# One attention unit programmed ahead, a third load slot, row sums from a column of ones, more small buffers

## The chip, the cores and the metric

One core of a Trainium2 chip runs the kernel as one program. The metric is device time in microseconds from the runs of the kernel; lower is better. The profile is of one execution. TensorE is PE in its rows (PEld its weight loads), VectorE DVE, ScalarE ACT, GpSimd POOL, SyncE SP; SP issues all the kernel's DMAs.

## The reference

Causal attention and a linear memory are mixed by a gate and fed to a two-layer network (called MoE in the code, with one expert). Shapes: B, H, S, D = 4, 8, 576, 64; 2304 tokens of 512 features; the hidden layer is 2048 wide.

```python
def _attn_ref(q, k, v, M_prev, z_prev, beta):
    scores = scale * np.matmul(q, k.transpose(0, 1, 3, 2))
    scores = np.where(causal, -1000000000.0, scores)
    scores = scores - scores.max(-1, keepdims=True)
    a = np.exp(scores)
    a /= a.sum(-1, keepdims=True) + 1e-09
    local = np.matmul(a, v)
    q_p = phi(q)                       # elu + 1
    mem_ret = np.einsum('bhsd,bhde->bhse', q_p, M_prev)
    mem_norm = np.einsum('bhsd,bhd->bhs', q_p, z_prev)[..., None] + 1e-06
    g = 1.0 / (1.0 + np.exp(-beta))[None, :, None, None]
    return g * (mem_ret / mem_norm) + (1 - g) * local

def reference(**kwargs):
    x = attn_out.transpose(0, 2, 1, 3).reshape(B * S, H * D)
    r = np.maximum(x @ w_in, 0.0)
    return (r * r) @ w_out
```

## The kernel before

All is float32 in and out; most matmuls run on float16 halves: a value is split into a high half and the rest, and a product takes three matmuls (high x high, high x low, low x high).

**Attention** runs in 24 units, in the order of the list `order`. A unit is one batch b, one pair of heads p and some query tiles. A tile is 128 queries (numbers 1 to 4); the first 64 tokens of each batch are handled apart at the start. Batches 0 and 1 have units of tiles 1 and 2 (four pairs), then of tiles 3 and 4 (four pairs); batches 2 and 3 have units of all four tiles. So units 0 to 7 are batch 0, 8 to 15 batch 1, 16 to 19 and 20 to 23 batches 2 and 3. A unit consists of a start and of rows.

The start: `loads` (L417, L421, L424) brings k, then q with the memory matrix (qm), then v (vv) into slots of which there are two each. q and k are split (qh, ql, kh, kl: L444 to L451), except in units 0 to 5, which use float32 scores; phi of q is made in place (L461 to L467). From unit 3 on v is scaled by a power of two that its largest absolute value gives: a maximum per partition (vx, L483), one small matmul that spreads it (vt, L487), a maximum and a reciprocal (vy, L488 to L492), vz (L493), and the split into vh and vl in the tile vs (L498, L500). Units 0 to 2 use v as it is. Then the memory product pm (L520), its norm (nm) and the first write of feat, the unit's 128 features of the tokens (L531). Then `after()` issues the loads of the next unit.

The rows, in the tile order 2, 1, 3, 4: scores (sp, L554, with a raised priority), a masked copy with the row minimum of the negated scores (e and mx, L575), the exponential (L595), which also sums its row into sm by the accumulator output, the split of the weights into float16 halves (a: L633 on ScalarE, L635 on VectorE), a transposing DMA (aT, L639), the factor of the row (sm times vz, reciprocal: L640, L644), the products with v (acc, L659), and the update of feat (L662). sm and mx have four buffers, vx, vy, vz and nm two.

PSUM is shared by names: up (2 buffers), acc (2), av (2) and s. vt, pm and the acc of attention all use the two av buffers.

Units above the fourth take their big tiles by turns from two pools, at for even units and the late pool (`more[-1]`) for odd ones, one buffer each of qh, ql, kh, kl, vs.

**MoE** runs in blocks of 256 tokens, `moe(n)`: up matmuls (L936 to L938), relu and square (L942, L943), the halves gh and gl (L945, L948), down matmuls (L908 to L910), output. Block 0 are the first tokens; blocks 1 to 6 follow; the tokens of the last two are done together in `moe_last` by a scheme of seven products (L782 to L784, L811). A block starts from `token_halves`: squares, scale and halves of feat (hl, two buffers) and a transposing DMA.

**What sets the order.** Each engine's queue is a fixed list. The program's order gives the priority, and a scheduler at build time lays the instructions out from it with modelled durations: an instruction later in the program can move forward when its inputs and its buffer are there. `ORD` writes attention units 0 to 3 merged with the weights' loading and conversion and with block 0, then units 4 to 23 one after the other, and behind these the MoE blocks; so MoE matmuls of a batch that is done fill TensorE beside later units. Within the attention part the program has a unit's start, its rows, the next unit's start, its rows.

## Time and profile before

| | us |
|---|---|
| runs of the kernel | 583.03, 586.88, 589.49 (median 586.88) |
| the profiled execution | 584.98 |
| its span, first to last instruction | 583.2 |
| TensorE busy | 535.7 (92%) |
| VectorE busy | 455.7 (78%) |
| ScalarE busy | 397.2 (68%) |
| GpSimd busy | 59.7 (10%) |
| mean granted TensorE clock, share of full | 0.97 |

A row of the waits gives the engine and line, what released it, the total, the number of waits and the longest. A busy TensorE is not one at its peak: its matmuls overlap, and their ends are modelled.

### The profile page before, as it was taken

How to read it: one execution, taken by the hardware profiler on the slowest of the kernel's cores; microseconds unless marked ns; L12 is line 12 of the kernel's file. 1: busy time of each engine (PE TensorE's matmuls, PEld its weight loads, DVE VectorE, ACT ScalarE, POOL GpSimd, SP SyncE). 2: the span in 40 equal slices, each digit the busy share in tenths (PEclk: the TensorE clock that was granted, in tenths of full speed). 3: DMA queues.
4: the chain of work that ended last, by engine and by line, in shares of the span. 5: the costliest groups of instructions: out<-in, count | busy, mean ns of one | idle time of the engine just before them, and what ended most of it. 6: DMA issues, size and time to landing. Idle time of an engine off the chain costs nothing.

```text
span 583.2 us, 12895 instructions
## 1 busy us (share of the span) xinstructions
PE 535.7 (92%) x4903; PEld 380.4 (65%) x4903; DVE 455.7 (78%) x1413; ACT 397.2 (68%) x853; POOL 59.7 (10%) x41
## 2 busy tenths in 40 slices
PE   6578997799799899999998999988999999999997
PEld 6466774576577576657765766656676776446766
DVE  6988779998687686889895775989767769795735
ACT  2566886777688677869787866889566664556452
POOL 2760674010010000000000000000000000000000
PEclk9968998699999999999998999999999999999999
DMA  8921886345865643767546846569454335100002
GB/s 308 404 89 38 281 320 164 90 100 121 157 128 117 143 118 91 158 136 174 123 108 104 196 74 118 117 122 178 64 114 86 79 57 71 38 0 1 2 1 72
DMA packets 131022, 70.87 MB, mean 122 GB/s; under 512 B 113296, under 2 KB 119440, under 8 KB 130960
## 3 DMA queue, kind: packets, MB, share of 16 engines
q1 hardware_dynamic: 130960, 70.05, 50.6%
q8 instruction: 38, 0.62, 0.5%
q14 instruction: 24, 0.20, 0.1%
HBM read 37.53 MB, written 4.72 MB: 72 GB/s over the span
## 4 chain that ended last, share of the span: by engine, by line
PE 35%; DVE 21%; ACT 12%; DMA 10%; issue 4%; SPq 1%; POOLq 0%; DVEq 0%; ACTq 0%
DVE a L635 4%; PE oacc L909 4%; PE oacc L908 4%; PE oacc L910 4%; PE up L938 4%; PE up L936 4%; PE up L937 4%; DMA qm<-in_qv_dram 3%; DVE e L575 3%; ACT e L595 3%; DMA vv<-in_qv_dram 3%; PE seven L811 3%; DMA aT<-a 3%; PE acc L659 3%; PE sp L554 2%
## 5 line engine op out<-in xcount | busy, mean ns | idle before, releaser
L936 PE MATMUL up<-xT,w 128*128 128x256 f16 x448 | 123.1, 275 | 1.2 <-ACT r L942 1.2
L937 PE MATMUL up<-xT,w 128*128 128x256 f16 x448 | 123.1, 275 | 0.3 <-DVE xT L397 0.3
L938 PE MATMUL up<-xT,w 128*128 128x256 f16 x448 | 123.2, 275 | 0.0
L595 ACT ACTIVATE e<-e,mx 128x320 f32<-128x320 f32 (+3 forms) x128 | 77.4, 606 | 46.3 <-DVE feat L662 27.4
L908 PE MATMUL oacc<-w,gh 128*128 128x512 f16 x224 | 85.5, 382 | 2.2 <-ACT gh L945 2.1
L635 DVE SCALAR_TENSOR_TENSOR a<-e,a 128x128 f16<-128x128 f32 x116 | 64.8, 569 | 27.3 <-ACT a L633 26.4
L909 PE MATMUL oacc<-w,gh 128*128 128x512 f16 x224 | 85.4, 381 | 0.0
L910 PE MATMUL oacc<-w,gl 128*128 128x512 f16 x224 | 81.0, 380 | 1.3 <-DVE gl L948 1.2
L633 ACT ACTIVATE a<-e 128x128 f16<-128x128 f32 x116 | 54.9, 523 | 3.9 <-DMA aT<-a 2.4
L659 PE MATMUL acc<-vs,aT 128*128 128x64 f16 x1138 | 46.3, 195 | 11.7 <-DMA aT<-a 7.2
L659 PEld LDWEIGHTS <-aT 128*128 128x128 f16 x1138 | 41.5, 99 | 20.8 <-DMA aT<-a 10.2
L937 PEld LDWEIGHTS <-w 128*128 128x128 f16 x448 | 44.3, 99 | 11.5 <-issue 1.5
L938 PEld LDWEIGHTS <-w 128*128 128x128 f16 x448 | 44.2, 99 | 9.2 <-issue 1.2
L936 PEld LDWEIGHTS <-w 128*128 128x128 f16 x448 | 44.2, 99 | 9.2
L575 DVE CUSTOM_DVE_ANT_0 e<-sp,mask 128x320 f32<-128x320 f32 (+3 forms) x128 | 47.0, 417 | 1.5 <-PE sp L554 1.0
L193 POOL TENSOR_SCALAR raw<-raw 128x512 uint32<-128x512 uint16 x21 | 44.8, 2134 | 21.4 <-DMA raw<-in_w_in_dram 12.8
L948 DVE TENSOR_TENSOR gl<-r,gh 128x512 f16<-128x512 f32 x56 | 39.4, 704 | 7.3 <-ACT gh L945 6.9
L942 ACT ACTIVATE r<-up,gam 128x512 f32<-128x512 f32 x48 | 32.3, 674 | 18.2 <-PE up L938 18.2
L910 PEld LDWEIGHTS <-gl 128*128 128x128 f16 x224 | 21.4, 98 | 23.5 <-DVE gl L948 3.4
L811 PEld LDWEIGHTS <-g 128*128 128x128 f16 x336 | 32.6, 98 | 6.0 <-DVE g L737 1.8
L908 PEld LDWEIGHTS <-gh 128*128 128x128 f16 x224 | 22.0, 98 | 22.1 <-ACT gh L945 2.7
L943 ACT ACTIVATE r<-r 128x512 f32<-128x512 f32 x56 | 34.9, 624 | 0.8
(196 smaller groups left out, 1076.1 us busy)
## 6 DMA issues: line engine op xcount, KB each, us to landing
raw<-in_w_in_dram SPq DMA_DIRECT2D x16, 512.0 KB, 7.1
raw<-in_w_out_dram SPq DMA_DIRECT2D x16, 512.0 KB, 7.9
vv<-in_qv_dram SPq DMA_DIRECT2D x16, 320.0 KB, 3.2
kd<-in_kk_dram SPq DMA_DIRECT2D x16, 288.0 KB, 3.2
out_dram<-o SPq DMA_DIRECT2D x12, 256.0 KB, 2.4
qm<-in_qv_dram SPq DMA_DIRECT2D x8, 321.0 KB, 3.4
qm<-in_qv_dram SPq DMA_DIRECT2D x8, 193.0 KB, 2.9
vv<-in_qv_dram SPq DMA_DIRECT2D x8, 192.0 KB, 4.7
```

What stands on the lines that cost most here:

```text
L575: nc.vector.tensor_tensor_reduce(out=e[:, h, ka:kb], in0=sps[:, h, cs], in1=mask[:, 448 - q0 + ka : 448 - q0 + kb], scale=-0.125, scalar=3 ...
L595: ex = nc.scalar.activation(e[:n, h, :ke], e[:n, h, :ke], AF.Exp, bias=bs, scale=-1.0, accum_out=sm[:n, h : h + 1])
L633: nc.scalar.mul(av[:, :, o0 : o0 + w], x, SC)
L635: nc.vector.scalar_tensor_tensor(out=av[:, :, o0 + w : o0 + 2 * w], in0=x, scalar=SC, in1=av[:, :, o0 : o0 + w], op0=ALU.mult, op1=ALU.sub ...
L659: nc.tensor.matmul(acc[:n, h], lhs[:, :n], rhs, start=x == 0, stop=x == len(mms) - 1)
L811: mms.append(nc.tensor.matmul(x[:, blk], g[j][:, i0, a, blk, p], t_side(j, p, m, i1), start=j == js[0] and p == n == 0, stop=j == js[-1] a ...
L908: nc.tensor.matmul(acc[t], gh[:, u, ts], w_out_op(f, 0), start=f == f0, stop=False)
L909: nc.tensor.matmul(acc[t], gh[:, u, ts], w_out_op(f, 1), start=False, stop=False)
L910: nc.tensor.matmul(acc[t], gl[:, u, ts], w_out_op(f, 0), start=False, stop=f == f1)
L936: nc.tensor.matmul(up[:, u, :], w_in_op(f, k, 0), xT[:, :, k], start=k == 0, stop=False)
L937: nc.tensor.matmul(up[:, u, :], w_in_op(f, k, 0), xT[:, :, NK + k], start=False, stop=False)
L938: nc.tensor.matmul(up[:, u, :], w_in_op(f, k, 1), xT[:, :, k], start=False, stop=k == NK - 1)
```

## The change

A unit's start of the program stands before the rows of the unit ahead of it: from unit 4 on (`FIRST`), `attn` runs the start of unit i + 1 up to a mark ("whole"), and then the rows of unit i. From unit 8 on (`AHEAD`) the loads go round three slots, the third one in the late pool, and from the start of unit 6 on loads are issued up to two units ahead instead of one. The tile of v (vs) has a column of ones behind vh, made once per pool; the products with vh are 65 columns wide and give the row sums, so that the exponential has no accumulator output except in units 0 to 2, and the factor sm is made after acc. The order of the three products changes. vx, vy, vz and nm get four buffers, mx and sm eight, hl four in the late pool; the last block's halves get tiles of their own.

```diff
-QB = 2
-VVB = 2
+LO = D + 2
-KB = 2
+AHEAD = 8
@@ before loads
+    def with_ones(ap):
+        if ap not in ones:
+            ones[ap] = ap.tile([P, 2, 5, LO + D], F16, tag="vs", name="vs", bufs=1)
+            nc.vector.memset(ones[ap][:, :, :, D : D + 1], 1.0)
+        return ones[ap]
-    def loads(b, p, tiles):
+    def loads(i):
+        b, p, tiles = order[i]
+        n = i % 2 if i < AHEAD else i % 3
+        lp = at if n < 2 else more[-1]
...
-        kd = at.tile([P, S], F32, tag="kd", name="kd", bufs=KB)
+        kd = lp.tile([P, S], F32, tag=f"kd{n}", name="kd")
...
-        qm = at.tile([P, 2 * ZW + SQ], F32, tag="qm", name="qm", bufs=QB)
+        qm = lp.tile([P, 2 * ZW + SQ], F32, tag=f"qm{n}", name="qm")
...
-        vv = at.tile([P, 5 * P], F32, tag="vv", name="vv", bufs=VVB)
+        vv = lp.tile([P, 5 * P], F32, tag=f"vv{n}", name="vv")
@@ attention (vx, vy, vz, nm: bufs=2 to bufs=4; mx, sm: bufs=4 to bufs=8)
-            nc.vector.tensor_scalar(out=vz, in0=gs[:, h0 : h0 + 2], scalar1=vy, scalar2=None, op0=ALU.mult)
-            vs = ap.tile([P, 2, 5, 2 * D], F16, tag="vs", name="vs", bufs=1)
+            nc.vector.tensor_scalar(out=vz, in0=gm[:, h0 : h0 + 2], scalar1=vy, scalar2=None, op0=ALU.mult)
+            vs = with_ones(ap)
...
-            vh, vl = (vs[:, :, :ncn, i * D : (i + 1) * D] for i in range(2))
+            vh, vl = (vs[:, :, :ncn, o : o + D] for o in (0, LO))
...
         after()
+        if ap_early:
+            yield "whole"
...
-                    e[:n, h, :ke], e[:n, h, :ke], AF.Exp, bias=bs, scale=-1.0, accum_out=sm[:n, h : h + 1]
+                    e[:n, h, :ke], e[:n, h, :ke], AF.Exp, bias=bs, scale=-1.0,
+                    **({"accum_out": sm[:n, h : h + 1]} if full else {}),
...
-            nc.vector.scalar_tensor_tensor(
-                out=sm[:n], in0=sm[:n], scalar=1e-9, in1=gm[:n, h0 : h0 + 2] if full else vz[:n],
-                op0=ALU.add, op1=ALU.mult,
-            )
-            nc.vector.reciprocal(sm[:n], sm[:n])
+            if full:
...
-            acc = ps.tile([P, 2, D], F32, tag="av", name="acc", bufs=2)
+            acc = ps.tile([P, 2, LO], F32, tag="av", name="acc", bufs=2)
...
-                    vh, vl = (vs[:, h, :, x * D : (x + 1) * D] for x in range(2))
+                    vh, vl = vs[:, h, :, : D + 1], vs[:, h, :, LO:]
...
-                        mms += [(low, vh[:, c]), (hi, vh[:, c]), (hi, vl[:, c])]
+                        mms += [(low, vh[:, c]), (hi, vl[:, c]), (hi, vh[:, c])]
...
+            if not full:
+                nc.vector.scalar_tensor_tensor(
+                    out=sm[:n], in0=acc[:n, :, D], scalar=SC * 1e-9, in1=vz[:n], op0=ALU.add, op1=ALU.mult
+                )
+                nc.vector.reciprocal(sm[:n], sm[:n])
@@ token_halves
-            hl = mo.tile([P, 2 * DM], F16, tag="hl", name="hl", bufs=2)
+            hl = more[-1].tile([P, 2 * DM], F16, tag="hl", name="hl", bufs=4)
@@ the units
+    def unit(i):
+        ld = nxt.pop(0)
+        def after():
+            while i + len(nxt) + 1 < min(len(order), i + (3 if i + 2 >= AHEAD else 2)):
+                nxt.append(loads(i + len(nxt) + 1))
+        ap = more[-1] if i > FIRST and i % 2 else at
+        early = i < NEF and max(order[i][2]) < 4
+        return attention(*order[i], ld, after, i < NEARLY, i < NES, early, ap, i >= FIRST)
     def attn(i0, i1):
+        ahead = []
         for i in range(i0, i1):
-            ld = nxt.pop()
-            def after():
-                if i + 1 < len(order):
-                    nxt.append(loads(*order[i + 1]))
-            yield from attention(*order[i], ld, after, ...)
+            rows = ahead.pop() if ahead else unit(i)
+            if i >= FIRST:
+                for x in (rows,) if i == FIRST else ():
+                    for _ in iter(lambda: next(x), "whole"):
+                        yield
+                if i + 1 < i1:
+                    ahead.append(unit(i + 1))
+                    for _ in iter(lambda: next(ahead[0]), "whole"):
+                        yield
+            yield from rows
```

## Rows read from the trace of the kernel before

**Rows 1.** Busy time by stage: length, PE, PEld, DVE, ACT, POOL, clock, DMA share, GB/s.

```profile
100.00:120.00 20.00, 14.91 (x111) 10.79 (x111) 19.76 (x63) 14.25 (x29) 1.41 (x1) 0.74 0.45 103
...
115.00:300.00 185.00, 176.14 (x1678) 124.92 (x1674) 151.37 (x538) 141.08 (x321) 6.85 (x6) 1.00 0.60 128
300.00:480.00 180.00, 169.72 (x1700) 121.31 (x1699) 135.46 (x492) 129.53 (x294) 0.00 (x0) 0.99 0.57 109
480.00:583.20 103.20, 98.46 (x654) 63.41 (x652) 71.33 (x103) 51.04 (x68) 0.00 (x0) 0.99 0.12 26
```

**Rows 2.** Waits of TensorE's matmuls, 115 to 500 us: total, times, longest.

```profile
PE acc L659 <- DMA aT<-a: 7.2, 5, 2.8
PE sp L554 <- DVE ql L445: 3.0, 3, 2.3
PE oacc L908 <- ACT gh L945: 2.1, 2, 1.6
PE acc L659 <- DVE mx L575: 1.6, 1, 1.6
PE oacc L910 <- DVE gl L948: 1.2, 2, 1.0
PE up L936 <- ACT r L942: 1.2, 2, 1.0
PE sp L554 <- DVE vx L485: 1.2, 1, 1.2
PE vt L487 <- DVE feat L662: 0.7, 1, 0.7
PE acc L659 <- DVE vs L500: 0.5, 2, 0.2
```

**Rows 3.** Chain that ended last, 198 to 204 us; VectorE's timeline at 354 us.

```profile
199.49 2.91 DMA qm<-in_qv_dram
...
202.86 0.44 DVE ql L445
...
354.73 0.82 DVE L483 TENSOR_REDUCE vx<-vv 128x1 f32<-128x640 f32 x1 [2.95 <-DMA vv<-in_qv_dram]
```

**Rows 4.** Waits of ScalarE and of SP's queue, 115 to 500 us.

```profile
ACT e L595 <- DVE feat L662: 27.4, 16, 3.2
ACT qh L444 <- DMA qm<-in_qv_dram: 20.8, 12, 2.9
...
SPq L421 <- PE pm L520: 17.1, 7, 8.2
```

**Rows 5.** Timeline, 284 to 321 us, units 16 to 18: start, duration, instruction.

```profile
284.36 0.82 DVE L483 TENSOR_REDUCE vx<-vv 128x1 f32<-128x640 f32 x1 [1.56 <-DMA vv<-in_qv_dram]
...
298.71 0.60 ACT L444 CAST qh<-qm 128x512 fp32r<-128x512 f32 x1
...
306.19 0.56 ACT L595 ACTIVATE e<-e,mx 128x320 f32<-128x320 f32 x1 [2.18 <-DVE feat L662]
...
315.37 0.48 DVE L662 SCALAR_TENSOR_TENSOR feat<-acc,sm,feat 128x64 f32<-128x64 f32 x2 [1.02 <-PE acc L659]
...
317.50 0.22 PE L487 MATMUL vt<-identb,vx 128*128 128x128 bf16 x1
...
320.04 0.83 ACT L498 ACTIVATE vs<-vv,vy 128x640 f16<-128x640 f32 x1
```

**Rows 6.** Groups of instructions (count, busy us, mean ns); landing of aT.

```profile
L659 PE MATMUL acc<-vs,aT 128*128 128x64 f16 x1138 | 46.3, 195 | 11.7 <-DMA aT<-a 7.2 <-DVE vs L500 2.6 <-DVE mx L575 1.6
...
L595 ACT ACTIVATION_READ_ACCUMULATOR e<-e,mx 128x1 f32 x108 | 20.3, 188 | 0.0
...
L662 DVE SCALAR_TENSOR_TENSOR feat<-acc,sm,feat 128x64 f32<-128x64 f32 x112 | 25.6, 276 | 5.5 <-PE acc L659 5.4
L640 DVE SCALAR_TENSOR_TENSOR sm<-sm,vz 128x2 f32<-128x2 f32 x56 | 6.3, 153 | 0.4
...
DMA to landing us min/median/max: 2.8/4.1/6.7
```

More of the change, by code (lines that the diff above doesn't have):

```diff
@@ L318, in first_tokens @@
             elif step == "l":
-                nxt.append(loads(*order[0]))
+                nxt.append(loads(0))
             elif step == "g":
@@ L412, in fused_kernel @@
     feat = {}
-    def loads(b, p, tiles):
+    ones = {}
+    def with_ones(ap):
[7 more added lines that the diff above has]
+        lp = at if n < 2 else more[-1]
         qa, qb = QT[tiles[0]][0], sum(QT[tiles[-1]])
-        kd = at.tile([P, S], F32, tag="kd", name="kd", bufs=KB)
+        kd = lp.tile([P, S], F32, tag=f"kd{n}", name="kd")
         nc.sync.dma_start(kd[:, :qb], kk_d[b, p, :, :qb])
-        qm = at.tile([P, 2 * ZW + SQ], F32, tag="qm", name="qm", bufs=QB)
+        qm = lp.tile([P, 2 * ZW + SQ], F32, tag=f"qm{n}", name="qm")
         qa, qb = qa - D + 2 * ZW, qb - D + 2 * ZW
@@ L425, in loads, with attention @@
         return kd, qm, vv
-    def attention(b, p, tiles, ld, after, early, sfull, full, ap):
+    def attention(b, p, tiles, ld, after, early, sfull, full, ap, ap_early):
         q_eng, k_eng = (nc.gpsimd if c == 'p' else nc.vector for c in (EARLY if early else LATE))
@@ L478, in attention @@
         if not full:
-            vx = at.tile([P, 1], F32, tag="vx", name="vx", bufs=2)
-            vy = at.tile([P, 1], F32, tag="vy", name="vy", bufs=2)
-            vz = at.tile([P, 2], F32, tag="vz", name="vz", bufs=2)
+            vx = at.tile([P, 1], F32, tag="vx", name="vx", bufs=4)
+            vy = at.tile([P, 1], F32, tag="vy", name="vy", bufs=4)
+            vz = at.tile([P, 2], F32, tag="vz", name="vz", bufs=4)
             vc = v[:, :ncn]
@@ L522, in attention @@
                     later("t", mm)
-            nm = at.tile([P, 3, 2], F32, tag="nm", name="nm", bufs=2)
+            nm = at.tile([P, 3, 2], F32, tag="nm", name="nm", bufs=4)
             pv = pm.rearrange("p i (h z) -> p i h z", h=2)[:, :ng]
@@ L568, in scores @@
                         ap.tile([P, 2, S], F32, tag="e", name="e", bufs=EB if ap is at else EB2),
-                        at.tile([P, 2, 2], F32, tag="mx", name="mx", bufs=4),
-                        at.tile([P, 2], F32, tag="sm", name="sm", bufs=4),
+                        at.tile([P, 2, 2], F32, tag="mx", name="mx", bufs=8),
+                        at.tile([P, 2], F32, tag="sm", name="sm", bufs=8),
                     )
@@ L639, in attention @@
                 nc.sync.dma_start_transpose(out=aT[:, :, :n], in_=a[:n])
[L640 to L644 removed]
+            if full:
+                nc.vector.scalar_tensor_tensor(
+                    out=sm[:n], in0=sm[:n], scalar=1e-9, in1=gm[:n, h0 : h0 + 2], op0=ALU.add, op1=ALU.mult
+                )
+                nc.vector.reciprocal(sm[:n], sm[:n])
             yield
[L647 removed]
+            acc = ps.tile([P, 2, LO], F32, tag="av", name="acc", bufs=2)
             for h in range(2):
@@ L656, in attention @@
                         hi, low = aT[:, h * nb + c], aT[:, h * nb + i + c]
-                        mms += [(low, vh[:, c]), (hi, vh[:, c]), (hi, vl[:, c])]
+                        mms += [(low, vh[:, c]), (hi, vl[:, c]), (hi, vh[:, c])]
                 for x, (lhs, rhs) in enumerate(mms):
-                    nc.tensor.matmul(acc[:n, h], lhs[:, :n], rhs, start=x == 0, stop=x == len(mms) - 1)
+                    nc.tensor.matmul(
+                        acc[:n, h, : rhs.shape[-1]], lhs[:, :n], rhs, start=x == 0, stop=x == len(mms) - 1
+                    )
+            if not full:
+                nc.vector.scalar_tensor_tensor(
+                    out=sm[:n], in0=acc[:n, :, D], scalar=SC * 1e-9, in1=vz[:n], op0=ALU.add, op1=ALU.mult
+                )
+                nc.vector.reciprocal(sm[:n], sm[:n])
             for h in range(2):
@@ L662, in attention @@
                 nc.vector.scalar_tensor_tensor(
-                    out=xo, in0=acc[:n, h], scalar=sm[:n, h : h + 1], in1=xo, op0=ALU.mult, op1=ALU.add
+                    out=xo, in0=acc[:n, h, :D], scalar=sm[:n, h : h + 1], in1=xo, op0=ALU.mult, op1=ALU.add
                 )
@@ L717, in moe_last @@
         ss, sc, osc, gam2 = (mo.tile([P, 4], F32, name=n) for n in ("ss4", "sc4", "osc4", "gam2"))
-        hs = [tl.tile([P, 2, DM], F16, tag="g", name="xh", bufs=3) if t < 2 else mo.tile([P, 2, DM], F16, tag="hl", name="hl", bufs=2) for t in range(4)]
+        hs = [tl.tile([P, 2, DM], F16, tag="g", name="xh", bufs=3) if t < 2 else tl.tile([P, 2, DM], F16, name=f"xh{t}") for t in range(4)]
         fb = feat[B - 1]
@@ L1005, in fused_kernel @@
     if not nxt:
-        nxt.append(loads(*order[0]))
+        nxt.append(loads(0))
+    def unit(i):
[6 more added lines that the diff above has]
+        return attention(*order[i], ld, after, i < NEARLY, i < NES, early, ap, i >= FIRST)
     def attn(i0, i1):
+        ahead = []
         for i in range(i0, i1):
-            ld = nxt.pop()
-            def after():
-                if i + 1 < len(order):
-                    nxt.append(loads(*order[i + 1]))
-            yield from attention(*order[i], ld, after, i < NEARLY, i < NES, i < NEF and max(order[i][2]) < 4, more[-1] if i > FIRST and i % 2 else at)
+            rows = ahead.pop() if ahead else unit(i)
[8 more added lines that the diff above has]
+            yield from rows
             b, p, tiles = order[i]
```

## The prediction

> **What bounds the kernel now.** I read the busy time by stage first, then TensorE's own waits, then who makes the other engines late. After 115 us the matrix engine is busy 95, 94 and 95% of three long stages; the next engine, VectorE, 82, 75 and 69% [rows 1]. The attention units run down to about 480 us, and the feed-forward (MoE) matmuls fill TensorE between their pieces. The reader is to see that attention finishing sooner is by itself worth nothing: matmuls that no longer run beside it run after it. What counts after 115 us is the time in which TensorE sits in front of a matmul whose input is late. From 115 to 500 us that is nine lines, 18.7 us together: 7.2 on transposes of the softmax weights (aT), 3.0 and 1.2 in front of scores, 2.1 and 1.2 and 1.2 in front of MoE matmuls, 1.6, 0.7 and 0.5 in front of products with v [rows 2]. The stage before, VectorE full at 19.76 of 20 us while the last weights are converted and TensorE at 14.91 [rows 1], is made of weights and of early units, which the change leaves as they are.
>
> Then the causes. The longest wait in front of scores ends a chain that starts with a load: qm is issued at 199.49, takes 2.91 us, and ql follows at 202.86 [rows 3]. At 354.73 VectorE has sat 2.95 us in front of vx, whose vv was loading [rows 3]; its queue goes in order, so the gl behind it is late too. Loads are late because SP holds a qm load until the second-last unit's pm has read the slot: 17.1 us in seven waits; ScalarE in turn is idle 20.8 us in front of qh for want of qm [rows 4]. ScalarE waits 27.4 us in front of the exponentials, released by a feat update of VectorE [rows 4]. An exponential needs no feat; it writes its row sums into sm, of which there are four, and the tile four earlier is read up to its feat.
>
> Last, the order within a unit. Unit 18 casts its q at 298.71, before unit 17's first exponential at 306.19: that half of a unit's start already runs a unit ahead. The half with v does not: unit 17 has its maximum at 284.36, but vt, with one small instruction between, comes at 317.50, just behind unit 16's last feat at 315.37, and v is split from 320.04 [rows 5]. vt, pm and acc share two PSUM buffers named av, which go round in program order, and a unit's vt stands there behind the earlier unit's acc.
>
> **The change part by part.** The sum is made against the profiled execution, 584.98 us (span 583.2, 1.8 around it); it is 1.9 below the median of the runs shown, 586.88.
>
> *Third slot, loads two units ahead.* The same loads, none added; they leave SP one unit sooner, because the slot they wait for was read a unit earlier. Behind a waiting load on SP stand the transposes, and behind those acc, so SP waits less in front of both. The waits for ql (3.0) and vx (1.2) go: −4.2. Of the 1.2 in front of MoE matmuls on gl, the longest stall, 1.0, is the one at 355 us: −1.0. Bounds: 0, if the load merely waits elsewhere, and −5.4.
>
> *A unit's start before the rows of the unit ahead of it.* No instruction is added; about a dozen of VectorE and ScalarE and, on TensorE, vt and pm move in front of the earlier unit's rows. acc waiting on vs (0.5) and vt waiting on feat (0.7) go: −1.2. Bounds: 0 and −2.8, with the 1.6 on mx, which I keep, because VectorE's rows now stand behind another unit's start.
>
> *Row sums by the ones column.* The 108 reads of the accumulator in the stage go: 20.3 us of ScalarE [rows 6]. ScalarE is not the bound (76 and 72% in the attention stages [rows 1]), so this gives nothing directly. With the four sm also gone as a brake (eight now, and written only after acc), the 27.4 us of waits go. What TensorE gets is part of its 2.1 and 1.2 us on gh and r, which queue behind those exponentials: I take half, −1.6; ends 0 and −3.3. A tile of number i has 2(2 + 3i) products, 2(1 + 2i) of them with vh; 13, 13, 16 and 16 tiles of i = 1 to 4 make 720 of the 1138 [rows 6]. They get a column more: 46.3 us over 1138 x 64 columns is 0.64 ns a column, +0.5. The two instructions on sm (153 ns the first [rows 6], the second much alike) move behind acc, which holds its PSUM buffer until two feat of 276 ns are done [rows 6]: 0.55 us becomes some 0.86. TensorE's only wait on feat was 0.7, so +0.4; if every one of 58 tiles paid, +18. The wait of VectorE for acc is no new one, feat stood there before.
>
> *More small buffers, four hl in another pool, persistent v tiles, two memsets.* No instruction but the memsets is added: nothing. The MoE matmuls cover them; uncovered, two memsets of 10 columns cost less than two feat updates of 64 (276 ns [rows 6]), 0.6 us.
>
> *What gets worse.* Units no longer chained run closer. VectorE at 75% from 300 to 480 us [rows 1] lets that stage shrink by a quarter at most; I take an eighth, half of it. Transposes come 1.14 times as dense, and the 7.2 us of waits on them grow by 1.0. Their landing takes 4.1 us in the median and 6.7 at most [rows 6], so the bad end is five waits longer by 2.6 us each, +13; the good end is that all 7.2 go.
>
> The Trainium skill speaks against this part ("DMA: Bandwidth & Descriptors", section on queues, rings and completion order): descriptors from SP are consumed in ring order on each DMA engine, so a transpose stands behind loads that were sent ahead of it. By that rule the +13 would be the nearer end, 591 in all; the median of 4.1 us, with loads in the same queue already, says that most transposes don't pay it, so 579 stands.
>
> Sum: −4.2 −1.0 −1.2 −1.6 +0.5 +0.4 +1.0 = −6.1. 584.98 − 6.1 is 578.9: 579 us, 1.3% under the median shown. From the median itself the same step gives 580.8, so the forecast stands near the edge of what can be told apart: about 1% (5.9 us) is what a measurement here can tell from no change.
>
> **The rivals.** *B, nothing moves.* The score half ran ahead already [rows 5], and TensorE's stalls come where the fixed order of its queue and the real arrivals differ; the same number appears at other places. For it: two of the nine lines, on aT and mx, are of a kind that is not touched, and they are 8.8 of the 18.7 us [rows 2]. Against: loads issued just in time are named in two chains. Time: 583 to 588, middle 586.
>
> *C, VectorE becomes the bound; slower.* With the chains cut, attention, first in priority, fills VectorE; gl of the MoE blocks comes late and TensorE idles beside it; the matmuls pushed back are then paid after attention. The price by the nearest row: from 100 to 120 us VectorE was at 19.76 and TensorE lost 5.1 of 20 us [rows 1]. If half of what is left of the last attention stage (135 us of VectorE work, so 68) runs like that, it costs 17: 579 + 17 = 596. It decides where a stretch has VectorE over some 95%; at the 82% of the stage from 115 to 300 us, TensorE loses only 8.9 of 185. That is what speaks against it: the fullest long stage loses no more than the others.
>
> The Trainium skill has a rule that points the same way ("Perfetto Trace Analysis", section Optimization Strategy): where the most-contended engine changes over time, interleaving the stages helps. Running attention apart from the MoE matmuls is the contrary; by it C would be the case. The trace bears it out only in the stretch of 100 to 120 us.
>
> *D, much faster.* If all nine waits go, aT's too because their tiles are ready a unit sooner, 584.98 − 18.7 + 0.9 = 567. Against: nothing in the change shortens a transpose, and acc is still placed close behind it.
>
> **How the numbers follow.** Chances: the forecast (575 to 584) 0.50, B 0.20, C 0.18, D 0.12. The likeliest has its own range, 575 to 584: lower end with the waits on mx, gh and r gone wholly (3.3 more), upper end with the loads' 5.2 not won. The range 568 to 593 leaves out most of C (0.13) and a sliver of D (0.05). Faster by over 1% (below 581.0): D whole and two thirds of the forecast, 0.46; slower (above 592.8) nearly all of C and a little of B's spread, 0.19; the rest, 0.35, within 1%.
>
> **What would show it.** Right: SP's waits on pm before qm loads nearly gone; no ScalarE idle before qh on qm and no VectorE idle before vx on vv; no exponential waiting on feat, no accumulator reads in units after the third; vt a unit before its acc; attention done well before 480 us; TensorE's waits from 115 us on down to about 12 us, mostly aT. Wrong: the same TensorE idle total at other lines (B); VectorE above 95% with MoE matmuls waiting on gl or gh (C); aT landing at 5 us and more with acc waiting on it (the bad end of the transposes). What would break the forecast most simply is TensorE idle that grows in the attention stages while those stages get shorter.

## The result, and the profile after

The kernel after takes 590.34 us in the median of its runs (587.34 to 592.37), the kernel before 583.11 beside it (580.38 to 589.49). The ratio is 1.013, with an interval of 1.0107 to 1.0152: slower by 1.3%, where 1% faster was forecast. The profiled execution has a span of 588.5 us, 5.3 more than before; the one before, against which the forecast was made (584.98 us), lies 1.9 above its kernel's median.

The page after has TensorE busy 539.8 us (535.7 before), VectorE 459.7 (455.7), ScalarE 388.6 (397.2) and GpSimd 60.0 (59.7). Next come the stages of the kernel after, with the columns of [rows 1]; the last two rows are pieces of the stage from 115 to 300 us.

```profile
100.00:120.00 20.00, 15.24 (x102) 10.79 (x103) 16.63 (x42) 10.67 (x18) 1.41 (x1) 0.66 0.48 84
115.00:300.00 185.00, 171.42 (x1599) 120.84 (x1598) 165.03 (x587) 144.35 (x289) 5.95 (x6) 0.96 0.67 143
300.00:480.00 180.00, 174.60 (x1737) 126.28 (x1735) 130.94 (x461) 118.85 (x222) 0.00 (x0) 1.00 0.52 99
480.00:588.50 108.50, 103.97 (x690) 67.06 (x687) 66.10 (x93) 50.30 (x66) 0.00 (x0) 1.00 0.05 15
180.00:200.00 20.00, 19.88 (x196) 15.43 (x197) 19.01 (x79) 19.55 (x48) 0.00 (x0) 0.92 0.63 132
240.00:260.00 20.00, 19.35 (x176) 13.82 (x177) 19.30 (x69) 17.68 (x36) 0.00 (x0) 0.91 0.70 142
```

Against [rows 1] the reader is to see two stages that moved in opposite directions. From 300 to 480 us TensorE is idle 5.4 us, where it was 10.3: the later attention stage moved as was forecast, by 4.9 us. From 115 to 300 us it is idle 13.6, where it was 8.9, and its mean clock fell from 1.00 to 0.96. The clock stands at its lower level (1.2 GHz) in four stretches of some 3.4 us there, and in none before; at half speed they cost about half their length, an estimate of some 6.7 us. VectorE went from 151.4 to 165.0 in the same stage: more of attention runs there. In idle time the two stages about cancel, 19.0 us where it was 19.2. The 5.3 us are for the most part TensorE's own busy time, 4.1 more for the same 4903 matmuls, which is where a lower clock shows.

These are TensorE's waits from 115 to 500 us after, with the columns of [rows 2].

```profile
PE sp L567 <- DVE mx L588: 7.2, 7, 1.8
PE vt L498 <- DVE feat L683: 2.8, 3, 1.2
PE oacc L931 <- DVE gl L969: 2.7, 2, 1.9
PE sp L567 <- ACT e L608: 1.5, 2, 1.1
PE oacc L931 <- DVE vy L500: 1.3, 1, 1.3
PE acc L673 <- DVE feat L542: 1.0, 1, 1.0
PE pm L531 <- DVE feat L683: 0.9, 2, 0.7
PE acc L673 <- DMA qm<-in_qv_dram: 0.6, 1, 0.6
PE sp L567 <- DVE vy L500: 0.3, 1, 0.3
PE oacc L929 <- ACT gh L966: 0.3, 1, 0.3
```

The ten lines come to 18.6 us; before, nine lines came to 18.7 [rows 2]. The lines are mostly others. All 7.2 us on the transposes aT are gone, and so are the waits on ql, vx and vs, and those on gh and r fell from 3.3 to 0.3; in their place stand 7.2 us of scores that wait for the masked copies (mx) to empty the one PSUM buffer s, and 3.7 us of vt and pm behind a feat.

Who waits on the other engines, 115 to 500 us after, answers to [rows 4]; the last line is VectorE's wait before vx.

```profile
ACT e L608 <- DVE mx L588: 34.7, 26, 3.0
...
ACT qh L455 <- DMA qm<-in_qv_dram: 6.7, 5, 2.3
...
SPq L432 <- PE pm L531: 15.1, 5, 6.0
...
DVE vx L494 <- DMA vv<-in_qv_dram: 15.1, 13, 2.0
```

The exponentials' 27.4 us on feat are gone, and in their place they wait 34.7 us on mx (13.2 before). ScalarE's wait for q fell from 20.8 to 6.7. VectorE's wait for v hardly fell (16.8 before in the same window).

### The profile page after: what moved, and what is told of

Same layout as the page of the kernel before. It is cut to its first block, busy times and chain, and to the rows that moved or that the text cites. A ratio compares the mean times of both kernels' runs of the same rounds, so it can differ in the third digit from the quotient of the medians.

```text
span 588.5 us, 12787 instructions
## 1 busy us (share of the span) xinstructions
PE 539.8 (92%) x4903; PEld 384.0 (65%) x4903; DVE 459.7 (78%) x1415; ACT 388.6 (66%) x737; POOL 60.0 (10%) x41
## 4 chain that ended last, share of the span: by engine, by line
PE 46%; DVE 20%; DMA 18%; ACT 11%; issue 3%; SPq 1%; POOL 1%; ACTq 0%; DVEq 0%
DMA vv<-in_qv_dram 6%; PE up L957 5%; DMA aT<-a 5%; PE up L959 4%; PE up L958 4%; PE oacc L930 4%; PE oacc L931 4%; PE oacc L929 4%; PE seven L832 4%; PE acc L673 4%; DVE e L588 3%; DVE a L649 3%; PE sp L567 3%; ACT a L647 2%; PE seven L804 2%
## 5 line engine op out<-in xcount | busy, mean ns | idle before, releaser
L957 PE MATMUL up<-xT,w 128*128 128x256 f16 x448 | 125.4, 280 | 0.0
L958 PE MATMUL up<-xT,w 128*128 128x256 f16 x448 | 125.3, 280 | 0.0
L959 PE MATMUL up<-xT,w 128*128 128x256 f16 x448 | 125.3, 280 | 0.0
L608 ACT ACTIVATE e<-e,mx 128x320 f32<-128x320 f32 (+3 forms) x128 | 72.8, 607 | 41.1 <-DVE mx L588 40.8
L647 ACT ACTIVATE a<-e 128x128 f16<-128x128 f32 x116 | 54.3, 523 | 18.7 <-DMA aT<-a 18.3
L958 PEld LDWEIGHTS <-w 128*128 128x128 f16 x448 | 45.1, 101 | 11.1 <-issue 0.6
L957 PEld LDWEIGHTS <-w 128*128 128x128 f16 x448 | 45.0, 101 | 11.0
L959 PEld LDWEIGHTS <-w 128*128 128x128 f16 x448 | 45.0, 100 | 7.6 <-issue 0.4
L673 PE MATMUL acc<-vs,aT 128*128 128x65 f16 (+1 forms) x1138 | 44.7, 196 | 3.2 <-DVE feat L542 1.6
```

The lines of the kernel that those rows point to most:

```text
L608: ex = nc.scalar.activation(e[:n, h, :ke], e[:n, h, :ke], AF.Exp, bias=bs, scale=-1.0, **({"accum_out": sm[:n, h : h + 1]} if full else {}),)
L647: nc.scalar.mul(av[:, :, o0 : o0 + w], x, SC)
L673: nc.tensor.matmul(acc[:n, h, : rhs.shape[-1]], lhs[:, :n], rhs, start=x == 0, stop=x == len(mms) - 1)
L957: nc.tensor.matmul(up[:, u, :], w_in_op(f, k, 0), xT[:, :, k], start=k == 0, stop=False)
L958: nc.tensor.matmul(up[:, u, :], w_in_op(f, k, 0), xT[:, :, NK + k], start=False, stop=False)
L959: nc.tensor.matmul(up[:, u, :], w_in_op(f, k, 1), xT[:, :, k], start=False, stop=k == NK - 1)
```

## The experiments

Each ratio is to runs of the kernel before beside it, with its 95% interval. Where tiles in flight are given, they were counted in the trace: tiles whose exponential has started and whose feat has not, averaged over time.

### One part at a time

Three theories stood at first. O: starting a unit before the rows of the one ahead packs attention densely, and VectorE becomes the bound. S: sums made from acc come too late. L: the third slot crowds SP's queue.

**Rows first, start after**, everything else of the change kept:

```diff
-            if i >= FIRST:
+            if i >= LEAD:    # LEAD = 99
```

> The changed kernel with the program's order undone alone: a unit's start stands behind the rows of the unit before it again; third slot, ones column and buffers stay. Theory O (the new order packs units 4 to 15 so densely that VectorE is the bound there: in the changed kernel it is busy 165.0 of 185 us from 115 to 300 us, against 151.4 before, and TensorE loses 13.6 us in idle and about 6.7 us in half clock there against 8.9 and 0): back to 581 to 585. Theory S (row sums behind acc make VectorE wait for TensorE: 11.2 us in six waits on acc): stays at 588 to 592. Theory L (a third load slot crowds SP): stays at 588 to 592.

Measured: 596.41 us, ratio 1.0252 (1.0191 to 1.0312). Undoing the order made it 1.2% worse, so theory O does not explain the loss: within the change the build with the order is the better one. None of the three theories had 596.

**Sums by the accumulator again**, everything else kept (the eight sm too):

```diff
-                    e[:n, h, :ke], e[:n, h, :ke], AF.Exp, bias=bs, scale=-1.0,
-                    **({"accum_out": sm[:n, h : h + 1]} if full else {}),
+                    e[:n, h, :ke], e[:n, h, :ke], AF.Exp, bias=bs, scale=-1.0, accum_out=sm[:n, h : h + 1]
...
-                    vh, vl = vs[:, h, :, : D + 1], vs[:, h, :, LO:]
+                    vh, vl = vs[:, h, :, :D], vs[:, h, :, LO:]
```

> The changed kernel with the row sums undone alone: the exponential gives them by its accumulator again, and sm is made before acc. Theory S: back to 581 to 585, VectorE's 11.2 us of waits on acc go back to about 5. Theory O: 589 to 592, since 20 us more of ScalarE come back and the density stays. Theory L: 588 to 592.

Measured: 590.77 us, ratio 1.0144 (1.0099 to 1.0190). The same as the kernel after, with the waits elsewhere: 4.9 us on aT again, 1.8 on mx. Theory S is not it.

**Two slots**, everything else kept:

```diff
-AHEAD = 8
+AHEAD = 99
```

> The changed kernel with two load slots and loads one unit ahead, all else as in it. Theory L: back to 581 to 585. Theory O: 588 to 594, the order is the same, and loads come later still. Theory S: 588 to 592.

Measured: 584.83 us, ratio 1.0046 (1.0009 to 1.0082). Taking the slot out gives back some 5 us, as L wants. It also tells against VectorE as the bound: the stage from 200 to 300 us is as full of VectorE as in the kernel after (88.2 and 88.7 of 100 us), and the kernel is 5 us faster.

**The order alone**, in the code of the kernel after with its other parts undone:

```diff
+            if i >= FIRST:
+                for x in (rows,) if i == FIRST else ():
+                    for _ in iter(lambda: next(x), "whole"):
+                        yield
+                if i + 1 < i1:
+                    ahead.append(unit(i + 1))
```

> The kernel before with the program's order alone: a unit's start ahead of the earlier unit's rows; two slots, accumulator sums, small tiles, hl and v tiles as before. Theory O: 588 to 594, and from 115 to 300 us VectorE at 88% or more with TensorE losing more than before's 8.9 us. Theories S and L: 579 to 584.

Measured: 589.31 us, ratio 1.0115 (1.0071 to 1.0160). That is O's time, but not its sign: VectorE is at 83% from 115 to 300 us (154.05 of 185), where O asked for 88%. So the order costs 1.2% alone and gives about 1% inside the change. The sign depends on what else is there, and parts that change sign need another kind of theory. From here on the rivals were R (the reshuffle: each engine's queue is laid out at build time by modelled durations, any edit lays it out anew, and a new order is worth some per cent either way), P or M (the parts have prices of their own), and several narrower ones.

**Everything undone in the code of after**, sums and counts of buffers as before too:

```diff
-AHEAD = 8
+AHEAD = 99
+LEAD = 99
...
-            vs = with_ones(ap)
+            vs = ap.tile([P, 2, 5, LO + D], F16, tag="vs", name="vs", bufs=1)
```

> The code of the kernel after with every part of the change undone: rows before the next start, two slots, sums by the accumulator, the old buffer counts. What is left of the new code is the layout of the slots' names, a v tile two columns wider without ones, and the order of the last two of the three products with v; the build-time queue may come out a little different. Every theory of a part expects 583 us, within 1 of the kernel before. Theory R (reshuffle: the queues are fixed at build time by modelled durations, so any edit moves TensorE's stalls, and the time of any new order of the queues is uncertain by some 1%) allows up to 6 us either way, and the width it shows here is the width with which the other runs must be read.

Measured: 585.33 us, ratio 1.0027 (0.9997 to 1.0057). What is left of the new code costs nothing that can be told. Its stages are the base for the runs that add one part to it:

```profile
115.00:300.00 185.00, 172.32 (x1639) 122.47 (x1638) 146.94 (x523) 136.68 (x311) 6.39 (x6) 1.00 0.61 126
300.00:480.00 180.00, 173.16 (x1719) 123.37 (x1717) 139.13 (x500) 133.41 (x302) 0.00 (x0) 0.99 0.56 113
```

**The third slot alone**, against the kernel with everything undone:

```diff
-AHEAD = 99
+AHEAD = 8
```

> The kernel before with the third slot and the loads two units ahead alone. Theory P (the third slot has a price of its own, loads collide with the transposes on SP's queue): 588 to 589 us, the 5.5 us that taking it out of the kernel after gave back, with more waits of acc on aT. Theory O (it only does harm together with the order, where attention already presses on VectorE): 579 to 583, the waits on ql, vx and qm gone. Theory R: anywhere from 578 to 590, not to be worked out from the other runs.

Measured: 578.54 us, ratio 0.9931 (0.9897 to 0.9965): faster than the kernel before, and 6.8 us faster than the kernel that it differs from by the slot alone. P, which took the slot's harm for its own, is refuted. Its stages, and TensorE's waits from 115 to 500 us:

```profile
115.00:300.00 185.00, 178.07 (x1686) 126.06 (x1684) 153.75 (x552) 144.90 (x325) 6.98 (x6) 0.99 0.65 137
300.00:480.00 180.00, 173.74 (x1720) 124.42 (x1719) 133.57 (x484) 127.85 (x291) 0.00 (x0) 0.99 0.58 105
```

```profile
PE acc L673 <- DMA aT<-a: 5.7, 5, 3.5
PE acc L673 <- ACT vs L510: 2.5, 1, 2.5
PE acc L673 <- DVE feat L543: 1.2, 2, 0.6
PE sp L568 <- DVE mx L589: 1.0, 1, 1.0
PE acc L673 <- DVE vs L512: 0.8, 1, 0.8
PE acc L673 <- DVE sm L658: 0.7, 1, 0.7
PE oacc L924 <- ACT gh L961: 0.5, 1, 0.5
PE vt L499 <- DVE feat L678: 0.4, 1, 0.4
PE up L952 <- ACT r L958: 0.2, 1, 0.2
```

The waits of scores on ql are gone (3.7 us with everything undone), and the waits come to 13.0 us in all, where they are 19.2 with everything undone. VectorE does not wait before vx at all (9.2 us with everything undone). The stages idle 6.9 and 6.3 us, against 12.7 and 6.8 with everything undone and 8.9 and 10.3 in the kernel before [rows 1].

**The ones column alone**, against the kernel with everything undone:

```diff
+            vs = with_ones(ap)
...
+                    **({"accum_out": sm[:n, h : h + 1]} if full else {}),
...
+                    vh, vl = vs[:, h, :, : D + 1], vs[:, h, :, LO:]
```

> The kernel before with the row sums from the ones column alone. In the three kernels with the ones column TensorE lost 7 to 11 us in front of scores on mx and little on aT; in the three with accumulator sums it was the other way. Theory Q (the ones column is what moves the stalls from aT to mx): sp on mx at 6 us or more here, acc on aT under 4, ScalarE without waits on feat. Time by Q alone: 583 to 587, as the two waits are of like size. Theory P: no change, 583. Theory R: 578 to 590.

Measured: 593.1 us, ratio 1.0148 (1.0093 to 1.0202). Q is right on where the waits stand (scores on mx 8.9 us, acc on aT 2.0, no exponential on feat) and wrong on the time, by 6 us at least. R's range ended at 590, so it was too narrow, here and in the next three runs.

**The buffers alone**, against the same (vx, vy, vz and nm likewise from two to four):

```diff
-                        at.tile([P, 2, 2], F32, tag="mx", name="mx", bufs=4),
-                        at.tile([P, 2], F32, tag="sm", name="sm", bufs=4),
+                        at.tile([P, 2, 2], F32, tag="mx", name="mx", bufs=8),
+                        at.tile([P, 2], F32, tag="sm", name="sm", bufs=8),
...
-            hl = mo.tile([P, 2 * DM], F16, tag="hl", name="hl", bufs=2)
+            hl = more[-1].tile([P, 2 * DM], F16, tag="hl", name="hl", bufs=4)
```

> The kernel before with the larger counts of small buffers (mx, sm 8 each; vx, vy, vz, nm 4 each; four hl in the late pool) alone. Theory Q': the eight sm already free the exponentials (27.4 us of ScalarE's waits on feat gone) and scores run ahead, so sp on mx appears here without the ones column. Theory Q: it doesn't, the accumulator sums still tie exponentials to ScalarE's order; time 581 to 584. Theory R: 578 to 590, and the four single parts don't add up to the whole change's 7.2 us.

Measured: 593.74 us, ratio 1.0154 (1.0099 to 1.0208). Scores wait on mx 4.4 us, so the freed sm does some of that without the column, as Q' has it; the exponentials' waits on feat are not gone, 9.8 us are left. Order, column and buffers cost 1.2, 1.5 and 1.5% alone and the slot gives 0.7: 3.5% by sum, where the whole costs 1.3. They don't add up.

### The four sm as a brake

In every kernel with four sm and accumulator sums the tiles in flight stand at 3.6 or 3.7 in the mean after 300 us and never above 4: the four sm hold the exponentials back. In the kernel after they are 9.6 from 300 to 350 us. Theory K made this the cause.

**Eight sm alone**, against the kernel with everything undone:

```diff
-                        at.tile([P, 2], F32, tag="sm", name="sm", bufs=4),
+                        at.tile([P, 2], F32, tag="sm", name="sm", bufs=8),
```

> The kernel before with eight sm instead of four, and nothing else of the change. In the five kernels so far with four sm and accumulator sums the tiles between their exponential and their feat are 3.6 in the mean and never above 4 from 150 us on: ScalarE waits 27 to 37 us for a feat. In the kernels with eight sm, or with the ones column, it is 6 to 9 tiles from 300 us on. Theory K (the four sm are a brake that keeps attention close together; without it scores and exponentials run ahead of the products with v, and TensorE waits on the masked copies): 590 to 594 us, the 9 of the buffers alone, sp on mx at 4 or more. Theory R (reshuffle; which buffer was grown does not matter): 578 to 590, no tie to sm.

Measured: 595.21 us, ratio 1.0225 (1.0162 to 1.0288). The time is a little over K's 590 to 594, and the waits on mx are as K wants (7.2 us). The place is only in part. Against the kernel with everything undone TensorE's busy time fell by 4.1 us from 115 to 300 us (172.3 to 168.2), where from 200 us on some 4 tiles are in flight (3.2 and 3.8 without), and by 2.3 from 300 to 480 us (173.2 to 170.9), with 6.4 to 7.4 in flight. More is lost before the tiles run far ahead than after.

**The buffers, but four sm**, against the buffers alone:

```diff
-                        at.tile([P, 2], F32, tag="sm", name="sm", bufs=8),
+                        at.tile([P, 2], F32, tag="sm", name="sm", bufs=4),
```

> All the larger counts of small buffers and the four hl in the late pool, but sm left at four. Theory K: the 9 us of the buffers alone are gone: 581 to 586 us, tiles between exponential and feat at most 4. Rival H (hl in another pool, or the eight mx, cost it): 590 to 594 as with eight sm. Theory R: 578 to 590.

Measured: 591.1 us, ratio 1.0172 (1.0123 to 1.0221), with at most 4 tiles in flight. The brake is on and the time is still 1.7% up: K falls as the cause of the buffers' price, and the time is in H's range. When the larger counts were built one by one, eight mx, or four of vx, vy, vz and nm, left every queue as it was; the only edits among them that change an order are the eight sm and the four hl in the late pool, and hl alone (with the tiles of the last block's halves) gives the queues of this run.

**The kernel after with accumulator sums and four sm**, against the run with the accumulator sums:

```diff
-                        at.tile([P, 2], F32, tag="sm", name="sm", bufs=8),
+                        at.tile([P, 2], F32, tag="sm", name="sm", bufs=4),
```

> The kernel after with the sums by the accumulator again and sm at four: third slot, order ahead and the other buffers stay. It differs from the earlier run that undid the sums alone (590.8) in the count of sm only. Theory K: 5 to 9 us less than that, 581 to 586, tiles between exponential and feat at most 4, waits on feat back at ScalarE. Theory O' (the order ahead costs 6 by itself whatever else is there, as it did alone): 585 to 589. Theory R: no less than 588.

Measured: 587.48 us, ratio 1.0103 (1.0043 to 1.0162). Some 3 us better than with eight, which is less than K's 5 and inside what the next runs show an order to be worth. Only O' has this time in its range, and the run with the rows first speaks against O'.

**The third slot and eight sm**, against the slot alone:

```diff
-                        at.tile([P, 2], F32, tag="sm", name="sm", bufs=4),
+                        at.tile([P, 2], F32, tag="sm", name="sm", bufs=8),
```

> The third slot alone (578.5) with eight sm beside it. Theory K: the brake's price is the same here: 585 to 590 us. Theory L' (the third slot and the loads two ahead feed a longer chain, so running ahead does no harm): 577 to 581.

Measured: 586.71 us, ratio 1.0092 (1.0060 to 1.0125): 8 us over the slot alone, as K has it, and 8.5 under eight sm alone. So the slot is worth as much here, and L' (577 to 581) is refuted. K has the times with eight sm alone and beside the slot for it; against it are the place of most of the loss in the first of these, and the buffers with four sm, which are as slow as with eight.

### Edits that do nothing

If R holds, an edit without any mechanism must cost as much. The bit mask on vx, an instruction on 128 x 1 that gives the same when repeated, was written twice in a single unit:

```diff
-            nc.vector.tensor_scalar(out=vb, in0=vb, scalar1=0x7F800000, scalar2=None, op0=ALU.bitwise_and)
+            for _ in range(1 + ((b, p, tiles) == order[5])): nc.vector.tensor_scalar(out=vb, in0=vb, scalar1=0x7F800000, scalar2=None, op0=ALU.bitwise_and)
```

In most units that leaves the order alone. In units 5, 6 and 8 (and, in the kernel after, 5 and 11) the queues of TensorE, VectorE, ScalarE and SyncE, which issues the loads, come out in another order from about there on. The first three are made in the code with everything undone.

> The kernel with every part undone (585.3, or 0.3% over the kernel before), and in unit 5 the bit mask on vx (a VectorE instruction on 128 x 1, idempotent) written twice. Its own cost is one instruction of 128 x 1, under 0.2 us. The build lays out the queues anew from unit 3 or 4 on. Theory R (the new order is what costs, whatever the edit; the kernel before is a good draw): 588 to 594 in two or three of the three nulls. Theory M (the parts have prices of their own): 583 to 586 in all three.

Measured: 595.51 us, ratio 1.0203 (1.0134 to 1.0272).

> The same null in unit 6. Theory R: 588 to 594 in two or three of the three nulls, TensorE's waits on other lines than in the kernel before. Theory M: 583 to 586.

Measured: 588.01 us, ratio 1.0085 (1.0050 to 1.0121).

> The same null in unit 8. Theory R: 588 to 594 in two or three of the three nulls. Theory M: 583 to 586.

Measured: 584.99 us, ratio 1.0040 (1.0003 to 1.0076).

So the kernel with one more instruction of about 0.15 us stands 0.4, 0.9 or 2.0% over the kernel before, according to the unit; the same code without it stands 0.3% over, so the instruction itself makes 0.1, 0.6 or 1.8%. Of the two theories M is refuted by the first; R asked for 588 to 594 in two of three, and got 588.0 and, above its range, 595.5. The stages of the first null, and its longest waits from 115 to 500 us:

```profile
115.00:300.00 185.00, 168.52 (x1577) 118.71 (x1575) 141.46 (x510) 132.45 (x302) 6.21 (x6) 0.97 0.64 124
300.00:480.00 180.00, 169.09 (x1706) 120.77 (x1705) 138.32 (x510) 132.80 (x303) 0.00 (x0) 1.00 0.57 115
```

```profile
PE acc L673 <- DMA aT<-a: 7.6, 7, 1.9
PE sp L568 <- DVE ql L457: 6.9, 3, 4.3
PE oacc L924 <- ACT gh L961: 2.1, 2, 1.8
PE sp L568 <- ACT qm L478: 2.0, 1, 2.0
```

TensorE's busy time from 115 to 300 us is 168.5, where it is 172.3 with everything undone and 176.1 before [rows 1]. The waits are of the kinds of before; the one on ql has grown from 3.7 us with everything undone to 6.9, and all of them from 19.2 to 27.0. The same work meets another order, and here it meets it badly.

**The third slot alone, with the null in unit 6** (AHEAD = 8, and the doubled mask):

> The third slot alone (578.5), with the same null in unit 6. Theory R: anywhere from 578 to 592, as the slot's 4 us were of the same kind. Theory M (the slot saves its waits on loads whatever the order): 577 to 581. Between the two: if the nulls on the kernel before come out at 588 to 594, the slot's own worth is the difference of this run to those, some 4 to 5.

Measured: 579.81 us, ratio 0.9921 (0.9892 to 0.9950). The slot keeps its gain in a new order: 8.2 us under the same null without it. No score waits on ql here either, and VectorE's wait before vx is 0.3 us (13.8 without the slot).

**The kernel after, with the null in unit 5 and in unit 11**, the doubled mask alone:

> The kernel after with the bit mask on vx of unit 5 written twice; everything else of the change stays. Theory R (the 7 us that the change costs are a draw of the order): a time well away from 590, most likely 580 to 588, since the nulls on the kernel before spread over 10 us. Theory M (the change as a whole has a price of its own, from attention running far ahead): 588 to 593, with scores on mx still the largest wait.

Measured: 584.39 us, ratio 1.0017 (0.9991 to 1.0043).

> The same null on the kernel after in unit 11, so the stage to about 240 us is left as in the kernel after and only what comes later is laid out anew. Theory R: a few us either way of 590, by half of what the unit-5 null moves or so, 582 to 594. Theory M: 588 to 593.

Measured: 586.9 us, ratio 1.0068 (1.0028 to 1.0108).

The whole change, with a doubled mask in one unit, is within 0.2% of the kernel before. Both times are under M's 588 to 593 and in R's ranges. Here are the stages of the null in unit 5, whose profiled execution is the slowest of its ten, and its longest waits from 115 to 500 us:

```profile
115.00:300.00 185.00, 170.38 (x1599) 118.19 (x1597) 161.48 (x579) 142.87 (x286) 6.12 (x6) 0.98 0.69 141
300.00:480.00 180.00, 176.44 (x1750) 126.99 (x1748) 136.98 (x475) 121.30 (x225) 0.00 (x0) 1.00 0.54 101
```

```profile
PE oacc L929 <- ACT gh L966: 4.0, 3, 1.9
PE sp L567 <- DVE mx L588: 3.7, 5, 1.1
PE oacc L931 <- DVE gl L969: 2.9, 3, 1.9
PE acc L673 <- DVE feat L542: 2.7, 3, 1.1
```

The tiles run ahead as in the kernel after (9.4 in flight from 300 to 350 us), TensorE has the late stage even fuller, the waits on mx are half, and the clock of the early stage is 0.98 instead of 0.96, though its idle time there is no less (14.6 us, 13.6 in the kernel after).

### What the runs settle, and what they leave open

| what is in the kernel | builds | ratios |
|---|---|---|
| nothing of the change, three of four with a null | 4 | 1.003, 1.004, 1.009, 1.020 |
| third slot alone, one of two with a null | 2 | 0.992, 0.993 |
| the whole change, two of three with a null | 3 | 1.002, 1.007, 1.013 |
| the slot with some of the other parts | 4 | 1.009, 1.010, 1.014, 1.025 |
| order, or column, or buffers, or sm, or buffers but sm, without the slot | 5 | 1.012, 1.015, 1.015, 1.017, 1.023 |
| everything but the slot | 1 | 1.005 |

Shown: a new order of the queues is by itself worth up to 1.8% here, so the 1.3% of the whole cannot be read as the price of its parts, and two of its three builds are within 0.7%. Likely, but not shown against a spread of that size: the third slot saves time. In three pairs of kernels that differ in the slot alone it is faster by 6.8, 8.2 and 8.5 us, each time with VectorE's wait before vx all but gone; in the fourth pair, inside the whole change, it is slower by 5.5. Not settled: what in the rest eats that gain in the kernel after. The seven builds that have the slot and more, the whole change among them, are all above the two with the slot alone, by 0.9 to 3.3%, where a null added up to 1.8; so some cost of the other parts is likely, but no run puts it on one of them. Nor is it known why taking the slot out of the whole change gave 5 us back. The kernel with the third slot alone beats both, at 578.5 us.

## Why the prediction was wrong

**What failed is the sum itself, in its way of counting.** It took nine waits of one profiled execution, struck those whose cause the change removes, and left the rest of the queue where it was. Every part of the change that was run by itself lays the queue out anew. That is rival B's sentence ("the same number appears at other places"), which got 0.20: 18.6 us of waits after, 18.7 before, other lines, where about 12 were foretold, mostly on aT; but B's time, 583 to 588, is missed too. The nulls show the size, up to 10 us (585.3 to 595.5), more than the whole sum of −6.1. So the forecast of 579 stood on differences smaller than the spread that an edit without any mechanism brings; it was off by 11 us. That its range of 568 to 593 holds the time is luck and no merit of the mechanism: 590 is the time of no rival, it lies between B's 588 and C's 596. Besides, the sum prices only waits. The waits came out even, and the profiled execution is 5.3 us longer all the same, 4.1 of them in TensorE's busy time. Of the five builds without any part of the change, the kernel before is the fastest, or level with the second, so that in these four a new order costs rather than gives; no view of one execution shows that.

**The third slot (−5.2)** has about its size by itself: −6.8 us against everything undone (−4.5 against the kernel before), −8.2 between two kernels with the same null, waits on ql gone, and VectorE's wait before vx with them. Inside the whole change it measured +5.5, and why is open. One sign of it was named wrongly: in the kernel after SP still holds qm loads behind pm (15.1 us, 17.1 before), but further ahead of need, and ScalarE's wait for qm falls to 6.7 us.

**The order (−1.2)** was right on its lines: acc waits on vs nowhere, and the last feat updates start at 462.79 instead of 473.18 us. Its other face was missed. vt and pm, which now stand between the earlier unit's acc in the round of the two av buffers, wait 3.7 us for a feat, where it was 0.7. That is the +0.4 for a buffer held longer, off by some 3 us in this execution; in the other builds with the order it is 0 to 2.5 us. And the lead that the slot gives to v is spent: VectorE waits 15.1 us before vx, where it waits not at all with the slot alone. The order is not the cause of that, since it is 15.9 us without the order and 5.1 with the order and accumulator sums. It comes back with the column; how is open. A piece of the timeline after shows what that does, VectorE's queue first, then TensorE's.

```profile
175.10 0.55 DVE L494 TENSOR_REDUCE vx<-vv 128x1 f32<-128x384 f32 x1 [1.24 <-DMA vv<-in_qv_dram]
...
177.71 0.68 DVE L969 TENSOR_TENSOR gl<-r,gh 128x512 f16<-128x512 f32 x1
```

```profile
176.17 0.38 PE L930 MATMUL oacc<-w,gh 128*128 128x512 f16 x1
178.44 0.39 PE L931 MATMUL oacc<-w,gl 128*128 128x512 f16 x1 [1.89 <-DVE gl L969]
```

This is the stall that the prediction priced at 1.0 for 355 us in the kernel before [rows 3]: a vx that waits for its load, a gl behind it in VectorE's queue, and MoE matmuls that wait for the gl. The forecast had it gone; here it is 1.89 us, at another place. The load accounts for at most 1.24 of it, since VectorE has some 2 us of other work between vx and gl.

**The ones column (−1.6 and +0.5).** The reads of the accumulator went (12 are left in the early units), the exponentials no longer wait on feat, and they run far ahead: the last starts at 433.2 us, 460.0 before. Of the waits on gh and r 3.0 of 3.3 us went, more than the half that was taken. But the exponentials now wait on mx (34.7 us, 13.2 before), and TensorE's scores wait there too, 7.2 us. The step asked what the exponentials hold up and not what would be late next in their own chain, the masked copies on VectorE, which share one PSUM buffer with the scores. The extra column cannot be seen: the 1138 products are busy 44.7 us after and 46.3 before [rows 6].

**More buffers (0).** Wrong in kind: an edit that adds no instruction was costed at nothing, and eight sm alone measured 2.3%, the buffers with four sm, whose order is that of hl alone, 1.7%. A buffer count is an input of the order, too. Costs like that belong in the range of every part, and the text had them in rival B alone.

**Denser transposes (+1.0)** came out the other way: their landing rose from 4.1 to 4.4 us in the median, and no wait of a TensorE matmul on aT stands in the list any more; with 9 tiles in flight they are ready well before acc. They hold up ScalarE instead, which waits 18.3 us (2.4 before) for a transpose to be done before it writes the next weights. The ring-order rule of the Trainium skill ("DMA: Bandwidth & Descriptors", section on queues, rings and completion order), which would have made this part +13, is not borne out as a price here: the landing moved by less than a tenth.

**A stage said to stay as it is** did not. Unit 3 stands in the stage where VectorE is full and makes its sums after acc now. The bulk of its acc starts at 104.27 (102.28 before), its feat only at 116.10 (106.31 before), and the next unit's vt at 120.03 (106.84 before). From the timeline of the kernel after, VectorE:

```profile
107.72 0.82 DVE L494 TENSOR_REDUCE vx<-vv 128x1 f32<-128x640 f32 x1 [1.13 <-DMA vv<-in_qv_dram]
...
112.39 0.15 DVE L677 SCALAR_TENSOR_TENSOR sm<-acc,vz 128x2 f32<-128x2 f32 x1
...
115.77 0.22 DVE L680 RECIPROCAL sm<-sm 128x2 f32<-128x2 f32 x2
...
116.10 0.85 DVE L683 SCALAR_TENSOR_TENSOR feat<-acc,sm,feat 128x64 f32<-128x64 f32 x4
```

The output of the first MoE block starts at 145.7 instead of 138.2 us. Whether these 7 us are worth anything is not shown: in the kernel with the column alone that feat is as late (115.33), and TensorE is full from 115 to 140 us all the same.

**Rival C** had its condition met, VectorE at 95 and 97% in two stretches of 20 us, and not its price: TensorE is busy 19.88 and 19.35 us in them, and the two-slot kernel is as full from 200 to 300 us and 5 us faster. The slowest build of all, with rows first and start after, has less VectorE from 115 to 300 us than the kernel after (155.9 and 165.0). C had the direction right, not the reason. The rule on interleaving ("Perfetto Trace Analysis", section Optimization Strategy, of the Trainium skill) is neither borne out nor refuted by these runs.

## What to carry to other kernels

Where a build lays the queues out from a model, a change of about 1% can be read only against nulls: repeat a harmless instruction in two or three places, and see how far the time moves before any part is credited or blamed. A part is then worth what it gives in several orders; the third slot was tried in four pairs here, and the fourth had the other sign. For a wait that is struck from a sum, the text has to say who is late next in the same chain, and for a buffer count it has to say whether it alters an order.

## What the runs showed of the hardware

A stall of TensorE can come with a cost beyond its length. After the 1.89 us in front of 178.44 the granted clock fell, in the kernel after:

```profile
176.40:178.40 2.00, 0.15 (x1) 0.00 (x0) 2.00 (x6) 0.00 (x0) 0.90 (x1) 1.00 0.49 91
179.80:183.20 3.40, 3.09 (x38) 2.95 (x39) 3.08 (x14) 3.40 (x11) 0.00 (x0) 0.51 0.61 161
```

The first row is the stall, with TensorE at 0.15 of 2.00 us; the second the stretch behind it, at 0.51 of full speed (the 1.2 GHz level), in which 3.09 us of busy time do the work of about half that. In the kernel after, the up matmuls of 256 columns follow each other after 0.21 us in another such stretch (241.84 and 242.05), and after 0.11 us at full speed, the 2.4 GHz level (299.56 and 299.67). So, by estimate, stall and clock together cost some 3.4 us and not 1.9. That the stall is the cause is not shown by an experiment, and the clock did not fall after every stall: after 1.77 us of idle time at 408 us the clock stayed at full speed. The prediction priced each wait at its length.
